# Matmuls of one array form put side by side, and the last weights and half of the output taken by column halves, in a kernel of windowed attention and soft experts

## The chip, the cores and the metric

The kernel runs on one core of one Trainium2 chip. A core has a matrix engine (TensorE, PE in the profile; its weight loads are the row PEld), a vector engine (VectorE, DVE), a scalar engine (ScalarE, ACT), a general engine (GpSimd, POOL) and SyncE (SP). Each works through its own list of instructions in order and waits on semaphores of the others. Matrix results go to PSUM, 8 banks of 512 float32 columns on 128 partitions; everything else lies in SBUF. Sixteen DMA engines move data between HBM and SBUF; loads are issued by GpSimd here (they turn float32 into float16 on the way), stores by SyncE. The metric is the device time of one execution in microseconds, the median of several runs.

## What is computed

Causal attention in a window of 64 keys (8 batches, 8 heads, 576 positions, 64 columns a head), and then a soft mixture of 8 experts with 4 slots each over the 4,608 rows of 512 that the attention gives. Cut to what matters:

```python
scores = scale * np.matmul(q, k.transpose(0, 1, 3, 2))
rel = pos[:, None] - pos[None, :]
scores = np.where((rel >= 0) & (rel < 64), scores, -1000000000.0)
attn = softmax(scores, axis=-1)
x = np.matmul(attn, v)                      # rows: 8 * 576, columns: 8 heads * 64
logits = x @ phi                            # [4608, 32]
d = softmax(logits, axis=0)                 # over all rows
slot_input = (d.T @ x).reshape(8, 4, 512)
for e in range(8):
    slot_out[e] = np.maximum(slot_input[e] @ w1[e], 0.0) @ w2[e]
c = softmax(logits, axis=1)
out = c @ slot_out.reshape(32, 512)
```

The inputs are float32: q, k and v 9.4 MB each, w1 and w2 16.8 MB each, and the output 9.4 MB.

## The kernel before, in words

The order of every engine is the order in which the program is written (`manual_schedule`), so what the code says first is done first on its engine.

**Attention.** The work is cut into 32 pairs of heads, p = 0 to 31, four pairs a batch. A loop over n = -1 to 30 ("slots", L515 to L585) works on several pairs at once, each in a different stage: the transposes of q of pair n and of k of pair n + 1 (`st_transpose`, L280), the row maxima of pair n - 1 (`st_max`, `st_max8`, L303 to L319), scores and exponentials of pair n - 2 (`st_scores`, L328 and L330; `st_score`, L335; `st_exp8`), products with v of pair n - 3 (`st_av`, L352) with their division (`st_norm`), transposes of the result of pair n - 4 (`fr_transpose`, L376). At the slot's end `st_shift` (L322) turns the maxima of pair n - 1, with 9 columns of m as its weights, and VectorE copies the rows into rt. ScalarE copies the turned k and q out of PSUM (L287, L292). Once a batch come the logits (`fr_logits`, L390), the running softmax over rows (`fr_max`, `fr_exp`, `fr_stat`), the slot sums (`fr_dispatch`, `fr_slots`, `fr_acc`) and the softmax over slots (`cb_max`, `cb_sub`, `cb_exp`, `cb_sum`, `cb_mul`, `cb_turn`), of which `cb_sub` and `cb_mul` run on GpSimd.

**Forms on TensorE.** A product with 128 weight columns uses the whole array. Products with 64 weight columns (the transposes of q and k, `st_av`) use half of its columns, those with 32 (logits, slots, experts) a quarter; the 9 columns of `st_shift` take a quarter too. The profile writes the form as rows*columns, such as 128*64.

**Loads.** All come from GpSimd, in one order (`loads`, L497): k, q and v in groups of two pairs (288 KB as float16), and the weights of experts 0 to 6, first matrices w1 (i = 0 to 6) and then second matrices w2 (i = 7 to 13), 1 MB each, by the table WSLOTS at L491: 12 of them in the loop, at n = 8i/3. v is copied once more by GpSimd, shifted by 64 rows (`shift_v`, L159 and L161), as soon as it has landed. Expert 7 has no place of its own: its first matrix is loaded in four quarters into buffers of q (`load_last1`, w1h), its second in four quarters into buffers of k (`load_last2`, w2h), each quarter two blocks of rows with all 512 columns.

**The tail** (from L618). After the loop the last pairs are finished. GpSimd there executes, in this order: the last w1h, `shift_v(15)`, the weights 12 and 13, four w2h, and `make_ss4` (L601), which writes a constant matrix ss4. `spread(b)` (L607) multiplies ss4 with the softmax over slots of batch b; `spread(0)`, in the middle of the tail, is followed on ScalarE by its copy and then by `fr_exp` of the last batch. Then come the last slot sums, and `first(g, f2)` (L741) multiplies the slot inputs by w1 of four experts at a time, `turn_hidden` turns the result, and `second(g, fcs)` (L763) multiplies it by w2, experts 0 to 3 (g = 0), then 4 to 7 (g = 1), into one PSUM bank `op`.

**The output.** ScalarE copies `op` to SBUF (osb, L806). Then, for each k of four quarters of the rows (two batches each), 9 products of 128 rows with 512 columns (L820) are copied out of PSUM by ScalarE and VectorE in turn (L821) and stored by SyncE (L823), three at a time, the first three singly. A partition's 9 rows lie one behind another in HBM.

Of the kernel before, what the change touches and what calls it, by code (L numbers as in the profile page):

```python
# [18 lines left out]
def kernel(  # L19
# [114 lines left out]
    def load_last2():  # L134
        i = len(w2_t[last])
        c = pin.tile([128, 2, D], FP16, name="w2h", tag="ks")
        nc.gpsimd.dma_start(out=c, in_=w2_dram(last)[:, i // 4, i % 4:i % 4 + 2, :])
        w2_t[last].extend(c[:, j, :] for j in range(2))
# [43 lines left out]
    NK, NQ = 3, 3  # L182
# [26 lines left out]

    make_rt(rts[0])  # L210
    zero_q(1)
    wm = const.tile([128, 5, 128], FP16, name="wm")
# [16 lines left out]
    phi_f = const.tile([128, NKK, NSLOT], FP32, name="phi_f")  # L229
# [41 lines left out]
    mts, xbs, pts, xts = {}, {}, {}, {}  # L271
# [14 lines left out]
    def st_copy_k(p):  # L286
        nc.scalar.activation(kTs[p % NK][:, 64:64 + S], turned(a_kh), AF.Copy, scale=QKS)  # L287
# [12 lines left out]
    def st_max(p):  # L300
        m = pw.tile([128, 10], FP16, name="m", tag="m")
# [6 lines left out]
        nc.vector.reduce_max(m[:, 0:8].rearrange("p (l c) -> p l c", l=2),  # L308
                             a_m[:, :, :].rearrange("p l (c x) -> p l c x", x=128), axis=AXX)
        mts[p] = m  # L310
# [7 lines left out]
    def st_max8_read(p, m8=m8):  # L318
        nc.vector.reduce_max(mts[p][:, 8:9], m8, axis=AXX)  # L319

    def st_shift(p, t_=a_v[64:64 + NB, 1, 384:512]):
        nc.tensor.matmul(t_, mts.pop(p)[:, 0:NB], ident_h[:, :], start=True, stop=True, skip_group_check=True)  # L322
        nc.vector.tensor_copy(out=rts[p % NR][64:64 + NB, :], in_=t_)  # L323
# [8 lines left out]
    def st_score(p):  # L332
        pt = pw.tile([128, NB, 128], FP16, name="pt", tag="pt")
        st_scores(p, range(8), lambda i: a_s[:, i // 4, 128 * (i % 4):128 * (i % 4) + 128])
        nc.scalar.activation(pt[:, 0:8, :].rearrange("p i x -> p (i x)"), a_s[:, :, :], AF.Exp, scale=XS)  # L335
        pts[p] = pt

    s8 = a_k[:, 288:416]

    def st_exp8(p):  # L340
        nc.scalar.activation(pts[p][:, 8, :], s8, AF.Exp, scale=XS)
# [62 lines left out]
    def fr_turn(b):  # L404
        pool = pw if b < B - 1 else pmo
        lgT = pool.tile([128, 6, 32], FP32, name="lgT", tag="lgT")
        nc.vector.transpose(lgT[:, :, :].rearrange("p i s -> p (i s)"), lgq[b][:, :])
        lgs[b] = lgT
# [15 lines left out]

    def cb_max(b):
# [10 lines left out]
    def cb_exp(b):  # L436
        pool = pw if b < B - 1 else pmo
        ec = pool.tile([128, 6, 32], FP32, name="ec", tag="lgec")
# [10 lines left out]
    def cb_mul(b, eng):  # L449
        ec, rs = cbs[b]  # L450
        pool = pw if b < B - 1 else pmo
        cc = pool.tile([128, 6, 32], FP16, name="cc", tag="cc")
# [35 lines left out]
    WSLOTS = {8 * i // 3: i for i in range(12)}  # L488
# [26 lines left out]
    for n in range(-1, NP - 1):  # L515
# [4 lines left out]
        if of(n, 17) is not None:  # L520
            cb_mul(of(n, 17), nc.gpsimd)

        if live(n - 1):
            st_max(n - 1)
            st_max8(n - 1)
        if live(n - 3):
# [3 lines left out]

        if live(n):
            st_transpose(n, "qs", a_qh)
            st_copy_q(n)
        if n == 0:
            masks_by_key()

        if sb is not None:
            fr_dispatch(sb)
            fr_dispatch_copy(sb)
        if live(n - 3):  # L540
            st_norm(n - 3)
        if sb is not None:
            fr_stat(sb)
        if eb is not None:
            fr_max(eb)

        if live(n - 2):
            st_score(n - 2)
        if live(n - 2):
            st_scores(n - 2, (8,), lambda i: s8)  # L550

        if sb is not None:
            fr_acc(sb, fr_slots(sb))
# [6 lines left out]

        if lb is not None:
            fr_logits(lb)
        if live(n - 4):
            fr_transpose(n - 4)
        if lb is not None:
            fr_logits_copy(lb)
        if live(n - 4):
            fr_transpose_copy(n - 4)
        if eb is not None:
            fr_exp(eb)  # L570
        if of(n, 15) is not None:
            cb_exp(of(n, 15))

# [52 lines left out]
    for i in range(12, 2 * NRES):  # L626
        load_w(i)
    for i in range(4):
        load_last2()
# [6 lines left out]
    st_shift(p - 1, a_k[64:64 + NB, 128:256])  # L636
# [6 lines left out]
    st_score(p - 1)  # L643
    st_max8(p, m8k)
# [4 lines left out]
    st_shift(p, a_m[64:64 + NB, 1, 384:512])  # L649
# [6 lines left out]
    st_score(p)  # L656
    st_scores(p, (8,), lambda i: s8)
# [68 lines left out]
    psr = ctx.enter_context(tc.tile_pool(name="psr", bufs=1, space=bass.MemoryType.PSUM))  # L726
    pex = ExitStack()
    psh = pex.enter_context(tc.tile_pool(name="psh", bufs=5, space=bass.MemoryType.PSUM))
    pso = pex.enter_context(tc.tile_pool(name="pso", bufs=1, space=bass.MemoryType.PSUM))
# [6 lines left out]
    op = pso.tile([128, D], FP32, name="op")  # L736
# [26 lines left out]
    def second(g, fcs):  # L763
        for fc in fcs:
            for j in range(4):
                nc.tensor.matmul(op[32 * j:32 * j + 32, :], hT[g][:, fc, 32 * j:32 * j + 32],
                                 w2_t[4 * g + j][fc], start=(g == 0 and fc == 0),
# [19 lines left out]
    second(0, range(4))  # L787
# [6 lines left out]
    second(0, range(4, 8))  # L794
# [5 lines left out]
    second(1, range(8))  # L800
# [5 lines left out]
    act(out=osb, in_=op[:, :])  # L806
    pex.close()
    obs = [w1_t[e, 0][:, 0:3, :].rearrange("p c f -> p (c f)").bitcast(FP32).rearrange("p (c d) -> p c d", d=D)
           for e in range(NRES)]
    pst = ctx.enter_context(tc.tile_pool(name="pst", bufs=2, space=bass.MemoryType.PSUM))  # L810
# [43 lines left out]
```

## Time and profile before

| what | value |
| --- | --- |
| runs | 195.84, 197.09, 197.68 us; median 197.09 |
| profiled execution | 196.56 us, its span 194.5 us, mean granted clock 0.962 |
| PE busy | 165.9 us, 85% of the span |
| ACT, DVE, POOL busy | 141.7, 137.0, 101.6 us |
| DMA | 40.87 MB as written, mean 210 GB/s; HBM read 61.93 MB, written 9.44 MB |
| chain that ended last | DMA 48%, POOL 13%, issue 10%, PE 9%, DVE 7%, ACT 5% |
| load of one weight (1,024 KB) | 16.0 us from issue to landing, median |
| k, q, v group (288 KB) | 10.7, 14.6, 12.8 us |
| last w2h issued, landed | 146.82, 164.31 us |
| first store issued | 166.65 us |

All times inside an execution count from the start of its span. The row DMA of the page's slices is the mean busy share of the sixteen engines; GB/s counts what is written, so a load of float32 that arrives as float16 counts half of what is read. The chain is followed back from the last instruction, each step to what released it. "Issue to landing" of a load includes the time in which it lies in the queue behind earlier ones. In a timeline a line is one group of instructions, with start, duration, engine, source line, operation, out<-in and shapes; a bracket tells how long the engine stood idle before it, and what ended that.

### The profile page before, as it was taken

The page shows a single profiled execution, that of the slowest core. Times are in us where ns is not written, and L with a number is a line of the kernel's source. Part 1 is how long each engine was busy: PE and PEld are TensorE (multiplying, and loading weights), DVE is VectorE, ACT ScalarE, POOL GpSimd, SP SyncE. Part 2 cuts the span into 40 slices and gives each one's busy share as a digit, 9 for nine tenths or more (in the row PEclk, how much of TensorE's full clock was granted, in tenths as well). Part 3 has the DMA queues.
Part 4 walks back from the last instruction along what each step waited for, and adds up shares of the span by engine and source line. Part 5 has one row for each costly group of instructions (what it writes and reads, how often), then busy time and mean ns, then how long its engine had stood idle before and what let it go on. Part 6 is the DMA issues. An engine that isn't in the chain of part 4 may idle for free.

```text
span 194.5 us, 6770 instructions
## 1 busy us (share of the span) xinstructions
PE 165.9 (85%) x2925; PEld 119.0 (61%) x2925; DVE 137.0 (70%) x325; ACT 141.7 (73%) x256; POOL 101.6 (52%) x131
## 2 busy tenths in 40 slices
PE   5599999979999999999999999999999898666100
PEld 1367878767777687777777777777785454232000
DVE  6676676857767877878887897878687756687400
ACT  4558878869788978979897987889878445556100
POOL 7959908289473736986456598547294133000000
PEclk9979999999999999999999999999999999999855
DMA  5999999999999999999999999999999993499993
GB/s 66 161 175 185 226 180 220 177 194 210 183 223 178 222 179 196 208 184 219 183 211 187 190 209 187 211 192 203 201 206 212 212 207 63 162 385 413 411 421 153
DMA packets 56573, 40.87 MB, mean 210 GB/s; under 512 B 38752, under 2 KB 51040, under 8 KB 55648
## 3 DMA queue, kind: packets, MB, share of 16 engines
q0 software_dynamic: 54000, 30.94, 113.3%
q1 hardware_dynamic: 2544, 9.50, 12.2%
q8 instruction: 23, 0.38, 0.7%
q14 instruction: 6, 0.05, 0.1%
HBM read 61.93 MB, written 9.44 MB: 367 GB/s over the span
## 4 chain that ended last, share of the span: by engine, by line
DMA 48%; POOL 13%; issue 10%; PE 9%; DVE 7%; ACT 5%; POOLq 0%; DVEq 0%; ACTq 0%
DMA v<-in_v_dram 31%; DMA w2h<-in_moe_w_dram 9%; DMA w<-in_moe_w_dram 6%; DVE w L821 5%; POOL v L161 3%; PE cp L820 3%; DMA qs<-in_q_dram 3%; POOL v L152 3%; POOL v L159 2%; POOL ks L79 2%; ACT qb L292 2%; PE a_m L306 1%; POOL qs L79 1%; PE a_m L303 1%; DVE m L308 1%
## 5 line engine op out<-in xcount | busy, mean ns | idle before, releaser
L292 ACT ACTIVATE qb<-a_q 64x576 f16<-64x576 f16 x64 | 41.3, 645 | 18.6 <-PE a_q L280 18.2
L308 DVE TENSOR_REDUCE m<-a_m 128x8 f16<-128x1024 f32 x32 | 39.2, 1224 | 12.6 <-PE a_m L306 12.1
L159 POOL COPY v<-v 64x1152 f16<-64x1152 f16 x16 | 18.3, 1141 | 42.9 <-DMA v<-in_v_dram 42.6
L335 ACT ACTIVATE pt<-a_s 128x1024 f16<-128x1024 f32 x32 | 32.8, 1024 | 1.1
L362 DVE TENSOR_TENSOR x_b<-a_v,rc 128x640 f16<-128x640 f32 x31 | 25.6, 824 | 1.1
L306 PEld LDWEIGHTS <-qb 128*128 128x128 f16 x256 | 17.2, 99 | 8.3 <-ACT qb L292 1.0
L287 ACT ACTIVATE kT<-a_k 128x576 f16<-128x576 f16 x32 | 20.9, 654 | 0.8 <-PE a_k L280 0.8
L380 ACT COPY xt<-a_q 128x576 f16<-128x576 f16 x31 | 20.4, 657 | 0.2 <-PE a_q L376 0.2
L306 PE MATMUL a_m<-kT,qb 128*128 128x128 f16 x256 | 19.9, 221 | 0.1
L152 POOL DMA_DIRECT2D v<-in_v_dram x16 | 19.9, 1241 | 0.0
L328 PE MATMUL a_s<-rt,lh 128*128 128x128 f16 x256 | 19.8, 220 | 0.0
L303 PE MATMUL a_m<-wm,ident_h 128*128 128x512 f16 x64 | 19.8, 391 | 0.0
L330 PE MATMUL a_s<-qb,kT 128*128 128x128 f16 x256 | 19.5, 219 | 0.0
L330 PEld LDWEIGHTS <-kT 128*128 128x128 f16 x288 | 18.8, 98 | 0.0
L328 PEld LDWEIGHTS <-lh 128*128 128x128 f16 x288 | 17.6, 98 | 1.7
L161 POOL COPY v<-v 64x1088 f16<-64x1088 f16 (+1 forms) x16 | 17.9, 1119 | 0.8
L323 DVE CAST rt<-a_v 9x128 f16<-9x128 f32 x30 | 8.7, 289 | 13.5 <-PE a_v L322 13.3
L280 PE MATMUL a_q<-ident_h,qs 96*64 96x96 f16 x384 | 14.8, 209 | 3.8 <-DMA qs<-in_q_dram 1.9
L352 PE MATMUL a_v<-v,pt 128*64 128x65 f16 x558 | 15.7, 197 | 1.4 <-POOL v L161 1.2
L280 PEld LDWEIGHTS <-qs 96*64 96x64 f16 x384 | 12.7, 111 | 5.7 <-issue 3.4
L352 PEld LDWEIGHTS <-pt 128*64 128x64 f16 x576 | 12.7, 110 | 4.6 <-issue 1.2
L280 PE MATMUL a_k<-ident_h,ks 96*64 96x96 f16 x384 | 14.8, 214 | 0.3 <-DMA ks<-in_k_dram 0.3
(162 smaller groups left out, 309.9 us busy)
## 6 DMA issues: line engine op xcount, KB each, us to landing
w<-in_moe_w_dram POOLq DMA_DIRECT2D x14, 1024.0 KB, 16.0
out_dram<-w SPq DMA_DIRECT2D x11, 768.0 KB, 8.1
qs<-in_q_dram POOLq DMA_DIRECT2D x16, 288.0 KB, 14.6
v<-in_v_dram POOLq DMA_DIRECT2D x16, 288.0 KB, 12.8
ks<-in_k_dram POOLq DMA_DIRECT2D x15, 288.0 KB, 10.7
w1h<-in_moe_w_dram POOLq DMA_DIRECT2D x4, 256.0 KB, 13.0
w2h<-in_moe_w_dram POOLq DMA_DIRECT2D x4, 256.0 KB, 17.3
out_dram<-w SPq DMA_DIRECT2D x3, 256.0 KB, 2.3
```

The costliest lines, as they stand in the source:

```text
L152: nc.gpsimd.dma_start(out=v1s[b % 2][:, c, 0:Dh], in_=v[b].rearrange("h s d -> (h s) d").rearrange("(c p) d -> p c d", p=128)[:, c, :])
L159: nc.gpsimd.tensor_copy(out=v2[64:128, c0:c1, 0:Dh], in_=v1[0:64, c0:c1, 0:Dh])
L161: nc.gpsimd.tensor_copy(out=v2[0:64, c0:c1, 0:Dh], in_=v1[64:128, c0 - 1:c1 - 1, 0:Dh])
L280: nc.tensor.transpose(tq[64 * hf:64 * hf + 64, RP * r:RP * r + RP], src[0:RP, h + hf, Dh * r:Dh * r + Dh], ident_h[0:RP, 0:RP])
L292: nc.scalar.activation(qbs[p % NQ][h, :, hf, :], turned(a_qh)[h], AF.Copy, scale=QKS)
L306: nc.tensor.matmul(a_m[:, i // 4, 128 * (i % 4):128 * (i % 4) + 128], qblock(p, i), kwindow(p, i), start=False, stop=True, skip_group_chec ...
L308: nc.vector.reduce_max(m[:, 0:8].rearrange("p (l c) -> p l c", l=2), a_m[:, :, :].rearrange("p l (c x) -> p l c x", x=128), axis=AXX)
L328: nc.tensor.matmul(at(i), lh[:, i, :], rt[:, :], start=(i % 4 == 0), stop=False, skip_group_check=True)
L330: nc.tensor.matmul(at(i), kwindow(p, i), qblock(p, i), start=False, stop=True, skip_group_check=True)
L335: nc.scalar.activation(pt[:, 0:8, :].rearrange("p i x -> p (i x)"), a_s[:, :, :], AF.Exp, scale=XS)
L352: nc.tensor.matmul(a_v[r0:r0 + 64, hf, 65 * (i // 2):65 * (i // 2) + 65], pt[:, i, 64 * hf:64 * hf + 64], rhs, start=True, stop=True, skip ...
L362: nc.vector.tensor_tensor(out=xbs[b][:, :, 128 * hp:128 * hp + 128].rearrange("p c (l d) -> p l c d", l=2), in0=avv[:, :, :, 0:64], in1=rc ...
```

## The change

In the loop the order of a slot's products is new. First come `fr_max`, `st_max` and `st_max8`, the score of the ninth block (now `st_score8`) and `fr_dispatch`; then the half-column products, `st_av`, the transposes of k and those of q; then (once a batch) the logits; and then whole ones, `st_score`, `fr_transpose` and `st_shift`, with `fr_slots` between them once a batch. `st_shift` takes all 128 columns of a wider m, whose other columns are zeros, so that it too uses the whole array. There are four buffers of kT instead of three, and every fourth k copy (p = 5, 9, ... 29) goes from ScalarE to VectorE. phi is first loaded into the place of w1 of expert 6, and some small tiles of the last batch lie in the place of lh.

The loop loads 10 weights, at n = 10i/3; the weights 10 to 12 come in the tail. The second matrix of expert 6 and that of expert 7 are loaded by column halves, in two pieces a half each: both experts' left halves, then both right halves. `second` works on one column half d at a time, in one PSUM bank each, first the experts 0 to 3 of both halves, then 4 and 5 of both, then 6 and 7. After 6 and 7 of the left half, the left half of the output of the first two quarters of the rows is computed and stored, then the right half in the same way; the other two quarters follow with whole rows.

```diff
-    def load_last2():
-        i = len(w2_t[last])
-        c = pin.tile([128, 2, D], FP16, name="w2h", tag="ks")
-        nc.gpsimd.dma_start(out=c, in_=w2_dram(last)[:, i // 4, i % 4:i % 4 + 2, :])
-        w2_t[last].extend(c[:, j, :] for j in range(2))
+    DH = D // 2
+    def load_half(d):
+        for h in range(2):
+            nc.gpsimd.dma_start(out=w2_t[last - 1, 0][:, 4 * h:4 * h + 4, DH * d:DH * d + DH],
+                                in_=w2_dram(last - 1)[:, h, :, DH * d:DH * d + DH])
+        w2_t[last].append([])
+        for h in range(2):
+            c = pin.tile([128, 4, DH], FP16, name="w2h", tag="ks")
+            nc.gpsimd.dma_start(out=c, in_=w2_dram(last)[:, h, :, DH * d:DH * d + DH])
+            w2_t[last][d].extend(c[:, j, :] for j in range(4))
...
-    NK, NQ = 3, 3
+    NK, NQ = 4, 3
...
-    phi_f = const.tile([128, NKK, NSLOT], FP32, name="phi_f")
+    phi_f = w1_t[NRES - 1, 0][:, 0, 0:2 * NKK * NSLOT].bitcast(FP32).rearrange("p (c s) -> p c s", s=NSLOT)
...
-        nc.scalar.activation(kTs[p % NK][:, 64:64 + S], turned(a_kh), AF.Copy, scale=QKS)
+        if p % 4 == 1 and p > 1:
+            nc.vector.tensor_scalar(out=kTs[p % NK][:, 64:64 + S], in0=turned(a_kh), scalar1=QKS, scalar2=None,
+                                    op0=ALU.mult)
+        else:
+            nc.scalar.activation(kTs[p % NK][:, 64:64 + S], turned(a_kh), AF.Copy, scale=QKS)
...
-    def st_shift(p, t_=a_v[64:64 + NB, 1, 384:512]):
-        nc.tensor.matmul(t_, mts.pop(p)[:, 0:NB], ident_h[:, :], start=True, stop=True, skip_group_check=True)
-        nc.vector.tensor_copy(out=rts[p % NR][64:64 + NB, :], in_=t_)
+    def st_shift(p, t_=a_v[:, 1, 384:512]):
+        nc.tensor.matmul(t_, ms[p % 2][:, :], ident_h[:, :], start=True, stop=True, skip_group_check=True)
+        nc.vector.tensor_copy(out=rts[p % NR][64:64 + NB, :], in_=t_[64:64 + NB, :])
...
-    WSLOTS = {8 * i // 3: i for i in range(12)}
+    WSLOTS = {10 * i // 3: i for i in range(10)}
...
-    for i in range(12, 2 * NRES):
+    for i in range(10, 2 * NRES - 1):
         load_w(i)
-    for i in range(4):
-        load_last2()
+    for d in range(2):
+        load_half(d)
     make_ss4()
...
-    psh = pex.enter_context(tc.tile_pool(name="psh", bufs=5, space=bass.MemoryType.PSUM))
+    psh = pex.enter_context(tc.tile_pool(name="psh", bufs=4, space=bass.MemoryType.PSUM))
...
-    def second(g, fcs):
-        for fc in fcs:
-            for j in range(4):
-                nc.tensor.matmul(op[32 * j:32 * j + 32, :], hT[g][:, fc, 32 * j:32 * j + 32],
-                                 w2_t[4 * g + j][fc], start=(g == 0 and fc == 0),
+    def second(d, g, js=range(4)):
+        for fc in range(NFC):
+            for j in js:
+                nc.tensor.matmul(ops[d][32 * j:32 * j + 32, 0:DH], hT[g][:, fc, 32 * j:32 * j + 32],
+                                 w2_at(4 * g + j, d, fc), start=(g == 0 and fc == 0),
...
+    def give(k, e0, ne, c0, nc_):
+        nonlocal turn, piece
         ov = out[2 * S * k:2 * S * k + 2 * S, :].rearrange("(p e) d -> p e d", e=NE)
...
+        for i0 in range(0, ne, n1):
+            n_ = min(n1, ne - i0)
+            cp = pst.tile([128, n1, nc_], FP32, name="cp", tag="cp")
...
+            (act, dve)[turn % 2](out=ob[:, i0:i0 + n_, :], in_=cp[:, 0:n_, :])
             turn += 1
...
+        nc.sync.dma_start(out=ov[:, e0:e0 + ne, c0:c0 + nc_], in_=ob)
+    second(0, 1, (2, 3))
+    act(out=osb[:, 0:DH], in_=ops[0][:, 0:DH])
+    for k, e0, ne in ((0, 0, 2), (0, 2, 2), (0, 4, 5), (1, 0, 4), (1, 4, 5)):
+        give(k, e0, ne, 0, DH)
+    second(1, 1, (2, 3))
+    act(out=osb[:, DH:D], in_=ops[1][:, 0:DH])
+    for k, e0, ne in ((0, 0, 4), (0, 4, 5), (1, 0, 4), (1, 4, 5)):
+        give(k, e0, ne, DH, DH)
+        spread(4 + 2 * k + e0 // 4, (act, dve)[turn % 2])
+    for k in range(2, B // 2):
+        for e0 in range(0, NE, 3):
+            give(k, e0, 3, 0, D)
```

## The prediction

> **What bounds the kernel now.** I read the page's slices first.
>
> ```profile
> PE   5599999979999999999999999999999898666100
> DMA  5999999999999999999999999999999993499993
> GB/s 66 161 175 185 226 180 220 177 194 210 183 223 178 222 179 196 208 184 219 183 211 187 190 209 187 211 192 203 201 206 212 212 207 63 162 385 413 411 421 153
> ```
>
> Each digit is 4.86 us. TensorE and the DMA engines are both full from about 5 to 160 us: the loads are a full pipe beside a full TensorE. Only near 160 to 170 us does the pipe run empty, before the output drains at about 410 GB/s. The chain of waits, from the last loads on:
>
> ```profile
> 134.53 12.01 DMA w<-in_moe_w_dram
> 146.53 0.28 issue
> 146.82 17.50 DMA w2h<-in_moe_w_dram
> 164.31 0.04 issue
> 164.36 0.61 PE op L766 x5
> 164.96 0.02 issue
> 164.99 0.59 ACT qb L806
> ```
>
> The end is set by the last load (164.31), but hardly: TensorE waited only 0.25 us for it. The first two lines matter more: a load issued at 134.53 lands at 146.53, and only then is the last w2h issued. The timeline of GpSimd (start, duration, what) shows the same:
>
> ```profile
> 142.84 1.41 POOL L122 DMA_DIRECT2D w<-in_moe_w_dram  x2
> 144.25 1.63 POOL L137 DMA_DIRECT2D w2h<-in_moe_w_dram  x3
> 146.82 0.54 POOL L137 DMA_DIRECT2D w2h<-in_moe_w_dram  x1 [0.94 <-DMA w<-in_moe_w_dram]
> 147.34 0.55 POOL L602 MEMSET v<- 128x512 f16 x1
> 147.95 1.33 POOL L605 COPY v<-ss 32x128 f16<-32x128 f16 x4
> ```
>
> GpSimd stood still for 0.94 us before its fourth w2h. The load that released it is the eighth before it in GpSimd's own order (w, w1h, w1h, w, w, three w2h). At 51.75 us a w load waits 0.47 us in the same way, for a q load eight before it. So at most eight of GpSimd's loads are under way; the ninth waits until the first has landed, and all of GpSimd waits with it. Behind these issues stand L602 and L605, make_ss4, ended at 149.28. The timeline of TensorE then has
>
> ```profile
> 148.97 0.42 PE L390 MATMUL a_s<-xt,phi_sb 128*32 128x128 f16 x8
> 149.31 0.43 PE L612 MATMUL a_v<-ct_all,v 128*128 128x128 f16 x5
> ```
>
> L612 is spread(0), which reads ss4: it starts 0.03 us after ss4 is complete. Whatever delays ss4 now delays TensorE, and all of the tail is behind it.
>
> **The change, part by part.** *Sorted products.* Same-form 128x128 matmuls start 56 ns apart; the start after a change of form comes 138 to 154 ns later, as in
>
> ```profile
> 88.26 0.45 PE L376 MATMUL a_q<-ident_h,x_b 128*128 128x128 f16 x5
> 88.64 0.22 PE L322 MATMUL a_v<-ident_h,m 128*9 128x128 f16 x1
> 88.80 0.61 PE L303 MATMUL a_m<-wm,ident_h 128*128 128x512 f16 x2
> ```
>
> (five starts at 56 ns would let L322 begin at 88.54; it begins at 88.64). A slot has six such changes (before and after L322; max to attention-value; transposes to score; score to k transposes; those to L376) and will have two. Four times about 95 ns is 0.38 us a slot of 4.37 us (the mean between the starts of L303), some 11 us over 30 slots. ScalarE gives up 7 k copies (0.65 us each), VectorE takes them. The loop then ends near 138 us instead of 149. This gain ends at spread(0), and what is late next there is ss4.
>
> *Weights in the loop: 10 instead of 12, five loads' worth behind it instead of three.* The same bytes cross the same full pipe; q, k and v only come earlier by two weights. Landings of a 1 MB weight are 4.9 us apart (154.4, then 159.3). Take w_5, the second matrix of expert 5. Ahead of it stand, before and after, the same loads: all of q, k, v, seven first matrices, w_0 to w_4 of the second, four w1h. In a full queue it lands when it landed before. It is the load issued at 142.84:
>
> ```profile
> DMA to landing us min/median/max: 11.6/11.6/11.6
> ```
>
> that is at 154.4. Take 154.4, with ends of 153.4 and 155.9 (uneven landings of the last loads).
>
> *Eight quarter loads instead of four.* After w_5, GpSimd issues w6a, w6a, w7a, w7a, w6b, w6b, w7b, w7b (experts 6 and 7, a and b the column halves). The eighth of them is the ninth load counted from w_5, and in the compiled order of the changed kernel it does wait on the semaphore that w_5 updates (the seventh on that of w_4). make_ss4 stays behind it. So GpSimd resumes at 154.4 + 0.29 (146.53 to 146.82), issues for 0.52, and make_ss4 takes 1.94 (147.34 to 149.28): ss4 is complete at 157.15 instead of 149.28. **spread(0) is 7.9 us later.** TensorE, done with attention at about 138, stands idle until then; ScalarE is queued behind spread(0)'s copy, with fr_exp of the last batch after it; GpSimd's cb_sub and cb_mul follow too.
>
> *Clock.* The granted clock was 0.50 at 10 to 12 us, after TensorE had been busy 0.48 of 2 us at 6 to 8, and L303's pair took 1.01 us there against 0.60. After some 18 us of idling spread(0) will meet that clock. The stretch from spread(0) to the first expert (149.31 to 155.18) holds about 3.7 us of matmuls that the path waits for. At half clock they cost up to 3.7 more; none if the clock returns at once. I take 2.5, as the slow stretch at the start lasted 3.4 us. The Trainium skill, "TensorE: Matmul & The Clock Gate", Part 1, says that an idle window of about 3.4 us halves the clock and a busy one restores it; by that rule alone 3.4 to 6.8 us would be slow and the term 2 to 3.7 us. The start of this trace agrees.
>
> *Second matrices by halves.* second(0) has the same columns. second(1) becomes three runs of about 0.9 us before half 0 is complete (pairs of experts, 16 matmuls of 256 columns), against two runs of 0.86: half 0 ends at 162.42 + 2.6 + 0.2 of latency = 165.2 on the old axis, against 164.97. **+0.2.** Its halves cover themselves: pieces of 768-byte runs (q, k) land 1.5 us apart for 288 KB, those of 128-byte runs (v) 2.0, so a 256 KB piece in 512-byte runs takes 1.33 to 1.8; half 0 is in by 159.7 to 161.6, half 1 by 168.8 at most, and they are wanted after 174.
>
> *First output.* 256 columns are copied from PSUM instead of 512, then one bank: about 1.35 us instead of 1.66 (164.99 to 166.65). **-0.3.**
>
> *Output.* Half of it now leaves in 1 KB runs. In the DMA records of the trace an output packet of 2,048 bytes takes 87 ns, one of 6,144 takes 240. By size alone 1 KB would be 43, no loss; by the ratio of the loads' 768- and 2,048-byte packets (80 and 173 ns) 50. At 48 ns, 4,608 packets on 16 engines are 13.8 us, against 11.7 for the same rows now: **+2.0** (0 to 2.6). By the Trainium skill, "DMA: Bandwidth & Descriptors", Specifications, 512 bytes are enough for line rate; by it this term would be 0 and the sum 2 us less. The trace's 87 ns against a third of 240 speaks for some loss already at 2 KB. Against this, the rows for 169 to 171 us show 217 and 227 GB/s instead of 410 (0.9 us lost to late copies); with four banks in turn **-0.8**.
>
> *No cost:* phi's place in w_6 (read at slot 5, loaded over at slot 20), the wider m and the fourth kT (the loop would have to lose 18 us to reach the path).
>
> Sum against the profiled run (span 194.5 us, 196.56 with what lies around it; the median of the three is 0.5 higher): 7.9 + 2.5 + 0.2 - 0.3 + 2.0 - 0.8 = 11.5, so **208.0 us**. With the ends: 196.56 + (6.9 + 0 + 0.2 - 0.3 + 0 - 1.0) = 202.4 and 196.56 + (9.4 + 4 + 0.2 - 0.3 + 2.6 + 0) = 212.5.
>
> **Rivals.** *1. The output starts under the last loads, and it is faster.* If ss4 were ready early, half 0 would be bound by its weights (159.7); first issue 161.6, first bytes 162.3, then 2.7 us left of the second halves, 24.9 of output (167.4 to 191.2 today, less 0.9, plus 2.0) and 3.3 to the end of the span: 193.2, or 195.3 us; if loads hide wholly under writes, 192.6. For it: the empty 164 to 167 us. Against it: the wait on w_5. It decides if the held issue waits for something that lands by about 146 us, w_3 rather than w_5.
>
> *2. The queue runs dry as well.* If the slots stay at 4.37 us (a latency or VectorE's k copies undo the gain), the last w1h still waits for TensorE until 139.1, while the queue, two weights shorter, empties at about 137.6 (the last v lands at 140.4 - 9.8; a w1h, a weight and a w1h follow, 1.2 + 4.9 + 1.2). Then shift_v (2.3), an issue, its way (1.7) and three weights: w_5 lands at 139.7 + 4.0 + 14.7 = 158.4, and all is some 4 us later: 212 us. Against it: the cost of a change of form is measured, and 0.1 us a slot brings that w1h to 136.
>
> *3. Sorting buys nothing on TensorE:* the same as rival 2 in time.
>
> **How the numbers follow.** Forecast 0.76, rivals 2 and 3 0.12, rival 1 0.09, 0.03 unplaced. Point 208, the forecast's. The range 202.4 to 212.5 is the forecast's own with both ends, and holds most of rival 2; rival 1 and the tails are left out, under 2 in 10. About 1% is what a measurement of this kernel can tell from no change (its runs span 195.84 to 197.68). Rival 1 divides into 0.05 faster and 0.04 same; of the unplaced, 0.01 each: faster 0.06, same 0.05, slower 0.89.
>
> **What would show it.** In the timeline of GpSimd a wait of some 10 us or more on a w load before the last w2h, ended at 154 to 155; make_ss4 after it; TensorE idle before spread(0) with Pool as releaser, and a granted clock of 0.5 there; the loads ended long before the first output. Starts of L303's successor near 4.0 us apart would show the sorting. I am wrong if the last w2h is issued before 148 us, or if writes and w2h loads overlap.

## The result, and the profile after

| | before | after |
| --- | --- | --- |
| median | 196.81 us (195.84 to 197.68, 4 runs) | 223.53 us (223.1 to 224.0, 4 runs) |
| ratio, 95% interval | | 1.136 (1.130 to 1.142) |
| span of the profiled execution | 194.5 us | 221.3 us |
| mean start to start of a slot, slots 4 to 28 | 4.37 us | 4.67 us |
| last w1h issued | 139.10 us | 149.59 us |
| w_5 (second matrix of expert 5) landed | 154.4 us | 171.29 us |
| ss4 complete | 149.28 us | 174.23 us |
| first store issued | 166.65 us | 193.35 us |
| first store to the end of the span | 27.85 us | 27.95 us |

The change is slower, as forecast, but by 26.7 us where 11.5 were forecast; the time lies 11 us above the upper end of the range. The page's slices of the kernel after (each digit 5.53 us) show the place:

```profile
PE   6599887889878788977988888899800599988300
PEclk9999999999999999999999999999955569999855
DMA  5999999999999999999999994396999990099996
GB/s 81 158 174 207 196 184 211 186 218 184 202 193 182 212 187 213 181 191 203 147 174 159 153 172 65 53 170 84 198 215 203 196 123 3 3 299 338 376 415 280
```

Two things are new beside the hole that was forecast (PE 00 near 160 to 171 us, the clock at half there and behind it, then a DMA hole while the experts run). TensorE stands mostly at 7 and 8 through the loop where it stood at 9. And the loads run dry before the loop is over: 65 and 53 GB/s from 133 to 144 us. The timeline of GpSimd (start, duration, engine, line, operation; in the bracket the idle time before it, and what ended that):

```profile
140.72 0.60 POOL L131 DMA_DIRECT2D w1h<-in_moe_w_dram  x1 [0.75 <-PE a_q L294]
141.31 0.72 POOL L122 DMA_DIRECT2D w<-in_moe_w_dram  x1
149.59 0.55 POOL L131 DMA_DIRECT2D w1h<-in_moe_w_dram  x1 [7.57 <-PE a_q L294]
150.19 1.14 POOL L169 COPY v<-v 64x1152 f16<-64x1152 f16 x1
151.38 1.14 POOL L171 COPY v<-v 64x1152 f16<-64x1152 f16 x1
152.47 2.13 POOL L122 DMA_DIRECT2D w<-in_moe_w_dram  x3
154.58 1.50 POOL L139 DMA_DIRECT2D w<-in_moe_w_dram  x2
156.07 1.48 POOL L144 DMA_DIRECT2D w2h<-in_moe_w_dram  x2
157.54 0.74 POOL L139 DMA_DIRECT2D w<-in_moe_w_dram  x1
161.52 0.74 POOL L139 DMA_DIRECT2D w<-in_moe_w_dram  x1 [3.24 <-DMA w<-in_moe_w_dram]
166.74 0.74 POOL L144 DMA_DIRECT2D w2h<-in_moe_w_dram  x1 [4.48 <-DMA w<-in_moe_w_dram]
171.58 0.74 POOL L144 DMA_DIRECT2D w2h<-in_moe_w_dram  x1 [4.10 <-DMA w<-in_moe_w_dram]
172.31 0.54 POOL L628 MEMSET v<- 128x512 f16 x1
172.91 1.32 POOL L631 COPY v<-ss 32x128 f16<-32x128 f16 x4
```

A w1h is a quarter of the first matrix of expert 7, a w a whole weight (L122) or a piece of half of expert 6's second matrix (L139), a w2h such a piece of expert 7's (L144). The lower half is the forecast stall: three of the eight pieces each wait for the load eight before them. These are w_3, w_4 and w_5, which landed at 160.74, 166.44 and 171.29, about 0.3 to 0.8 us before each issue; and make_ss4 stands behind them. The upper half is what was not forecast. The last w1h needs a buffer that the q transposes (L294) release, and they come so late that GpSimd waits 7.57 us for them, with three whole weights behind it in its list and only one weight left in the queue (issued at 141.31, landed at 152.26). The view of waits (who <- whom: us in total, times, longest) shows both ends of it:

```profile
PE a_q L401 <- ACT qb L310: 13.8, 21, 0.9
PE a_v L638 <- POOL v L631: 13.3, 1, 13.3
POOL w1h L131 <- PE a_q L294: 13.2, 4, 7.6
```

The second row is spread(0) waiting for ss4. The first is the loss in the loop: 21 times the transposes of the attention result wait for the copies of q. A slot's middle in the timeline of TensorE, and ScalarE at the same time:

```profile
84.07 0.61 PE L347 MATMUL a_s<-qb,kT 128*128 128x128 f16 x8
85.52 0.44 PE L401 MATMUL a_q<-ident_h,x_b 128*128 128x128 f16 x5 [0.84 <-ACT qb L310]
```

```profile
83.65 0.64 ACT L305 ACTIVATE kT<-a_k 128x576 f16<-128x576 f16 x1
84.18 1.29 ACT L310 ACTIVATE qb<-a_q 64x576 f16<-64x576 f16 x2
```

The q transposes fill bank a_q, and the result's transposes overwrite it. Before, the score, the ninth block and the k transposes stood between the two writes in TensorE's list, and ScalarE copied q first and k behind the score. Now only the score lies between, 16 starts at 56 ns or 0.90 us, and ScalarE copies k before the two halves of q. The copies end at 85.47, L401 starts at 85.52.

What the sorting did to TensorE itself is read from the busy times of the stretch 60 to 130 us, before and then after (the last row of the view by windows, four windows together):

```profile
sum 70.00, PE 68.97 PEld 53.29 DVE 57.01 ACT 61.40 POOL 44.67; mean PE 17.24 PEld 13.32 DVE 14.25 ACT 15.35 POOL 11.17
```

```profile
sum 70.00, PE 58.68 PEld 47.27 DVE 54.27 ACT 56.09 POOL 42.83; mean PE 14.67 PEld 11.82 DVE 13.57 ACT 14.02 POOL 10.71
```

Four slots take 17.43 us before and 18.86 on average after (18.7 or 19.0), so the 70 us hold 16.06 and 14.85 slots. TensorE works 4.29 us a slot before and 3.95 after: 0.34 of the 0.38 that the forecast priced is there. But it stands idle for 0.06 us a slot before and for 0.76 after, so that a slot grows by 0.36. Of the 11.3 us of idle in this stretch the view of waits names 6.8 as waits of L401 for the q copies (11 times), 2.9 as waits of L401 for the copy of the logits, which lies in the same bank (4 times), and 1.2 as waits of L321 for fr_acc on VectorE (4 times).

### The profile page after: what moved, and what is told of

It is laid out like the page before. It is cut to its first block, busy times and chain, and to the rows that moved or that the text cites. A ratio compares the mean times of both kernels' runs of the same rounds, so it can differ in the third digit from the quotient of the medians.

```text
span 221.3 us, 6986 instructions
## 1 busy us (share of the span) xinstructions
PE 163.9 (74%) x3007; PEld 123.3 (56%) x3007; DVE 142.0 (64%) x346; ACT 140.7 (64%) x263; POOL 105.0 (47%) x134
## 4 chain that ended last, share of the span: by engine, by line
PE 35%; ACT 19%; DMA 14%; DVE 12%; issue 10%; POOL 4%; DVEq 0%; ACTq 0%; POOLq 0%
ACT qb L310 11%; DMA w<-in_moe_w_dram 8%; PE a_m L321 5%; PE a_m L324 5%; PE a_v L377 4%; ACT kT L305 3%; DMA out_dram<-w 3%; PE a_k L294 3%; PE a_q L401 3%; DVE x_b L387 3%; DMA ks<-in_k_dram 2%; PE op L796 2%; ACT pt L366 2%; DVE m L326 2%; PE a_k L616 2%
## 5 line engine op out<-in xcount | busy, mean ns | idle before, releaser
L310 ACT ACTIVATE qb<-a_q 64x576 f16<-64x576 f16 x64 | 41.1, 642 | 5.7 <-PE a_q L294 3.2
L401 PE MATMUL a_q<-ident_h,x_b 128*128 128x128 f16 x155 | 13.7, 218 | 18.2 <-ACT qb L310 13.8
L366 ACT ACTIVATE pt<-a_k 128x128 f16<-128x128 f32 x32 | 8.9, 277 | 26.3 <-PE a_k L294 19.4
L401 PEld LDWEIGHTS <-x_b 128*128 128x128 f16 x160 | 11.2, 96 | 22.5 <-issue 22.0
L321 PE MATMUL a_m<-wm,ident_h 128*128 128x512 f16 x64 | 19.9, 394 | 1.7 <-DVE acc L512 1.5
L324 PE MATMUL a_m<-kT,qb 128*128 128x128 f16 x256 | 20.4, 225 | 0.1
L345 PE MATMUL a_s<-rt,lh 128*128 128x128 f16 x256 | 20.3, 223 | 0.0
L405 ACT COPY xt<-a_q 128x576 f16<-128x576 f16 x31 | 19.7, 635 | 0.2 <-PE a_q L401 0.2
L347 PE MATMUL a_s<-qb,kT 128*128 128x128 f16 x256 | 19.6, 220 | 0.0
L347 PEld LDWEIGHTS <-kT 128*128 128x128 f16 x288 | 19.0, 99 | 0.0
L294 PE MATMUL a_q<-ident_h,qs 96*64 96x96 f16 x384 | 15.9, 213 | 2.6 <-DMA qs<-in_q_dram 2.6
L305 ACT ACTIVATE kT<-a_k 128x576 f16<-128x576 f16 x25 | 16.1, 645 | 2.2 <-PE a_k L294 2.2
L294 PE MATMUL a_k<-ident_h,ks 96*64 96x96 f16 x384 | 16.2, 215 | 0.1
```

Source lines behind the costliest of these rows:

```text
L294: nc.tensor.transpose(tq[64 * hf:64 * hf + 64, RP * r:RP * r + RP], src[0:RP, h + hf, Dh * r:Dh * r + Dh], ident_h[0:RP, 0:RP])
L310: nc.scalar.activation(qbs[p % NQ][h, :, hf, :], turned(a_qh)[h], AF.Copy, scale=QKS)
L321: nc.tensor.matmul(a_m[:, j, :], ident_h[:, :], wm[:, j:j + 4, :].rearrange("p c x -> p (c x)"), start=True, stop=False, skip_group_check= ...
L324: nc.tensor.matmul(a_m[:, i // 4, 128 * (i % 4):128 * (i % 4) + 128], qblock(p, i), kwindow(p, i), start=False, stop=True, skip_group_chec ...
L345: nc.tensor.matmul(at(i), lh[:, i, :], rt[:, :], start=(i % 4 == 0), stop=False, skip_group_check=True)
L347: nc.tensor.matmul(at(i), kwindow(p, i), qblock(p, i), start=False, stop=True, skip_group_check=True)
```

## The experiments

The theory from the traces (T1): the new order of a slot makes TensorE wait for ScalarE, so the loop is slower. With two weights fewer in the loop the queue runs empty, the last w1h is issued late, and w_5 with it. ss4 then waits for w_5 (eight loads under way). The rivals: VectorE's share of the k copies slows the slots; the pipe is full and the table does not matter; the halves and 1 KB stores cost the time. Unless a run below says otherwise, its edit is to the changed kernel. Each is one execution with a profile, but for e10 and e11, and each is compared with a run of the kernel before on the same chip (196.55 to 197.27).

**e1: make_ss4 ahead of the loads.**

```diff
     st_transpose(p, "qs", a_qh)
+    make_ss4()
     load_last1()
...
         load_half(d)
-    make_ss4()
```

> The changed kernel with make_ss4 put ahead of the tail's last loads, nothing else. If the eight-loads limit holds ss4 and ss4 holds TensorE: the 13.3 us wait before spread(0) is gone, and with it the half clock; TensorE reaches spread(0) near 160 us, half 0 is then bound by its weights, which land at 176.6 as in the changed kernel (the loads do not move), first store near 179 instead of 193.4, and the rest (28 us from the first store to the end, plus the 3 us of right halves still to be loaded) gives a span of 207 to 211, a time of 209 to 213 us. If something else holds the tail, the time stays at 223.

Measured: 206.87 us, span 205.1, 2 us below what was expected. The loop is as slow as it was (4.67), w_5 lands at 169.28; GpSimd's three waits on weights are all still there, but nothing that TensorE waits for stands behind them, and the granted clock stays full until 195.1 us. The first store is issued at 176.80. So the place of make_ss4 behind the loads is worth 16.7 us of the 26.7, and 10 us have another cause.

**e2: slots in the order of before.** The loop body is that of the kernel before, every k copy on ScalarE; the table of 10, the halves, the wide m of `st_shift` and the late ss4 stay.

```diff
         if live(n - 3):
             st_av(n - 3)
         if live(n - 1):
             st_max8_read(n - 1)
-        if n == 0:
+        if live(n):
             st_transpose(n, "qs", a_qh)
             st_copy_q(n)
...
-        if live(n) and n > 0:
-            st_transpose(n, "qs", a_qh)
```

> The changed kernel with the loop's order of the kernel before, and all k copies on ScalarE; the tail, the load table, the halves and the wide m stay. If the new order in the slot is what slows the loop: slots back at 4.37 us (or a little less, as the wide m saves two changes of form, 0.2 us), the last w1h waits until about 139 (or 133), w_5 lands at 155 to 159 instead of 171.3, and the time is 207 to 212 us. If the loop is slowed by the load table or by the tail: slots stay near 4.67 and the time near 223.

Measured: 213.91 us, span 212.1, w_5 at 160.61, first store at 184.11. The slots are back at 17.41 us for four; the shift in whole-array form, alone, gains 0.02 in four slots. Yet this shift takes two of the four changes of form out and leaves the order as it was. TensorE's busy time in 60 to 130 us does fall, from 68.97 to 66.82 us or by 0.14 us a slot (two changes were priced at 0.19), but TensorE then waits, where the kernel before showed no wait:

```profile
PE a_q L294 <- ACT xt L405: 2.7, 8, 0.3
```

So in the old order, too, TensorE's work alone did not set the length of a slot. Bank a_q holds the transposes of the result, ScalarE's copy of them (xt) has to end before the q transposes may overwrite them, and ScalarE copies q after that. The kernel before already has it, in three of four slots, though its view of waits is empty:

```profile
89.82 0.66 ACT L380 COPY xt<-a_q 128x576 f16<-128x576 f16 x1
89.89 0.50 PE L352 MATMUL a_v<-v,pt 128*64 128x65 f16 x18
90.53 0.45 PE L280 MATMUL a_q<-ident_h,qs 96*64 96x96 f16 x12
```

The copy ends at 90.48, the q transposes start 0.05 us later. Of the time since the products with v, 0.50 us count as busy, so only 0.14 us of idling are left to see.

The new order of the slots costs 9.6 us in this setting. The time lies 2 us above what was expected, since even at the old pace the queue runs dry, as GpSimd's timeline shows:

```profile
138.79 0.55 POOL L131 DMA_DIRECT2D w1h<-in_moe_w_dram  x1 [7.30 <-PE a_q L294]
139.39 1.14 POOL L169 COPY v<-v 64x1152 f16<-64x1152 f16 x1
140.58 1.14 POOL L171 COPY v<-v 64x1152 f16<-64x1152 f16 x1
141.67 2.13 POOL L122 DMA_DIRECT2D w<-in_moe_w_dram  x3
```

The last w1h goes out when it did before the change (139.10), but up to w_5 three weights are behind it instead of one, and by then the one load ahead of it is about to land.

**e3: the result's transposes ahead of the attention-value products.**

```diff
+        if live(n - 4):
+            fr_transpose(n - 4)
+            fr_transpose_copy(n - 4)
         if live(n - 3):
             st_av(n - 3)
...
             fr_stat(sb)
-        if live(n - 4):
-            fr_transpose(n - 4)
-            fr_transpose_copy(n - 4)
```

The logits move up with them, ahead of the transposes.

> The changed kernel with the transposes of the attention result (and the logits before them) moved to the front of the slot, ahead of the products with v; the number of changes of form stays as in the changed kernel, or one more in the slot with logits. If TensorE waits because these transposes share PSUM bank a_q with those of q, whose two copies of 1.2 us come just before them in the changed order: the wait of 0.84 us a slot for qb goes, slots fall to 3.9 to 4.2 us, w_5 lands at 154 to 157 and the time is 205 to 209 us, with the wait on ss4 still there. If ScalarE or VectorE is simply full: slots stay above 4.5 and the time at 218 to 224.

Measured: 224.61 us, w_5 at 172.15, slots 4.73 on average: missed by 16 us. L401's wait for the q copies is gone, and slots without batch work fall to 3.6 to 4.1, but the slots with it grow to 5.7 to 5.8. New waits stand there: `st_max` for fr_acc, `st_shift` for the division on VectorE, the maxima for the q copies of the same slot. Time and slots are those given for a full ScalarE or VectorE, but neither works all the time: 56.0 and 54.2 us of the 70 from 60 to 130 us. Taking one wait out of the order puts another in.

**e4: all k copies on ScalarE.**

```diff
-        if p % 4 == 1 and p > 1:
+        if False:
             nc.vector.tensor_scalar(out=kTs[p % NK][:, 64:64 + S], in0=turned(a_kh), scalar1=QKS, scalar2=None,
```

> The changed kernel with all k copies on ScalarE again. If the bank a_q and the q copies set the pace: a copy of k of 0.54 us stands before the q copies in one slot more of four, so that slots grow by up to 0.13 us on average and the time is the same or up to 5 us more (223 to 228). If VectorE, with its seven k copies, sets the pace: slots fall to 4.3 or 4.4 us and the time to 210 to 214.

Measured: 223.89 us, slots 4.67, L401's wait 14.3 us (13.8). VectorE's k copies are not the cause.

**e5: q turned and copied before k.** In the sorted slot the logits and the q transposes come first, then exp8 and the q copies, then the k transposes, the dispatch copy and the k copy.

```diff
-        if live(n + 1):
-            st_transpose(n + 1, "ks", a_kh)
+        if lb is not None:
+            fr_logits(lb)
+        if live(n) and n > 0:
+            st_transpose(n, "qs", a_qh)
         if live(n - 2):
             st_exp8(n - 2)
-        if live(n + 1):
-            st_copy_k(n + 1)
...
         if live(n) and n > 0:
             st_copy_q(n)
         if lb is not None:
             fr_logits_copy(lb)
+        if live(n + 1):
+            st_transpose(n + 1, "ks", a_kh)
+        if sb is not None:
+            fr_dispatch_copy(sb)
+        if live(n + 1):
+            st_copy_k(n + 1)
```

> The changed kernel with another order inside the half-column part of a slot: logits, q transposes and their copies first, then k transposes and the k copy; the dispatch copy ahead of the k copy. The transposes of the attention result stay behind the scores, on bank a_q. If their wait for the q copies (0.84 us a slot) slows the loop: the q copies now run beside k transposes and scores (1.4 us), the wait falls under 0.2 us, slots fall from 4.67 to 3.8 to 4.1 us, the queue stays full, w_5 lands at 154 to 157, and the time is what was forecast for the changed kernel, 204 to 210 us, with ss4 still held until w_5 has landed. If the loop is slowed by something else in the new order: slots above 4.4, time 216 to 224.

Measured: 217.78 us, w_5 at 165.24, first store at 188.00. One slot in its timeline of TensorE:

```profile
63.00 0.61 PE L347 MATMUL a_s<-qb,kT 128*128 128x128 f16 x8
63.75 0.44 PE L401 MATMUL a_q<-ident_h,x_b 128*128 128x128 f16 x5
```

The end of L347 to L401 shrinks from 0.84 to 0.14 us, and a slot without batch work from about 4.4 to 3.7. That is the wait of T1, most of it taken out: ScalarE's q copies now end at 63.70, and from the last start of L347 to L401 there are still 0.36 us where products of one form follow each other at 0.056. The batch slots stay long (5.02 and 5.15), since they wait for other things: 0.47 us for the logits' copy, 0.40 for fr_acc. Four slots take 17.97 us, still more than the 17.43 of the order before. Of the 13 to 19 us expected, 5.7 came, and the time lies where it was put for a loop slowed by something else as well.

**e6 and e7: e5 and e2, each with make_ss4 ahead of the loads** (the edit of e1).

> The same, with make_ss4 ahead of the tail's last loads. If both causes are what I take them for, they add: TensorE passes spread(0) before 145 us; GpSimd is still held by the last two loads until w_5 has landed (155), ScalarE waits there for cb_sub of batch 5, then some 7 us to half 0; first store near 163, time 193 to 197 us. If the stall on ss4 was hiding another one as long: 203 us or more.

> The changed kernel with the slot order of the kernel before (as in the second experiment: 213.9 us, w_5 at 160.6, left halves in at 166) and make_ss4 first. If ss4 is the tail's only hold: half 0 is bound by its weights at 166 and TensorE's own chain at 165 to 167, first store at 168 to 169, time 197 to 200 us. If the lane wait also costs through cb_sub and cb_mul: up to 204.

Measured: e6 202.52 us (w_5 164.83, last piece of half 0 at 170.19, first store 172.36), e7 198.65 us (160.85, 166.22, 168.39). e7 is as expected; e6 is 5.5 us above, because the loop of e5 is too slow for it (w_5 was expected at 155). In both, the first store follows the last piece of half 0 by 2.17 us, and in e1 too (174.63, 176.80): with ss4 out of the way the loads set the end, and they follow the pace of the loop.

**e8: the kernel before, with make_ss4 ahead of its loads** (the same edit).

> The kernel before with make_ss4 ahead of its tail's loads. In its profile ss4 was complete 0.03 us before TensorE used it, and its wait on the eighth load back was 0.94 us. If ss4 was just in time there: no gain, 196 to 197 us. If it already held TensorE: up to 1 us faster.

Measured: 197.11 us, beside it 197.27. In the kernel before, ss4 was just in time.

**e9: the load table of before.**

```diff
-    WSLOTS = {10 * i // 3: i for i in range(10)}
+    WSLOTS = {8 * i // 3: i for i in range(12)}
...
-    for i in range(10, 2 * NRES - 1):
+    for i in range(12, 2 * NRES - 1):
```

> The changed kernel with 12 weights in the loop again (n = 8i/3) instead of 10; slots, halves and make_ss4 behind the loads as changed. Theory (the slots set when the last w1h is issued, and the queue is empty by then): slots stay at 4.67, the last w1h is issued near 149 as before, but one weight instead of three stands between it and the quarters, so w_5 lands where w_3 landed, at 161 to 163 instead of 171.3; the span is w_5 + 50 to 51.5, the time 213 to 216. Rival (the pipe is full, the same bytes take the same time wherever the table puts them, and something else held w_5): w_5 stays at 170 to 172, 222 to 225 us.

Measured: 211.58 us, span 209.8, slots 4.67, last w1h issued at 148.07, w_5 at 158.98. The theory holds in kind; w_5 lands 2 us earlier than it said, and the time is 1.4 us below its range. The rival of the full pipe falls: the table alone is worth 12.0 us. With e2 and the two kernels this fills a table of when w_5 landed:

| | 12 weights in the loop | 10 weights in the loop |
| --- | --- | --- |
| slots of before, 17.4 us for four | 154.4 | 160.61 (e2) |
| slots of the change, 18.7 to 19.0 us for four | 158.98 (e9) | 171.29 |

The pace alone makes it 4.6 us later, the table alone 6.2, both 16.9: 6.1 more than the sum (4.1 by e1, where w_5 landed at 169.28 with the slots and the table of the change). The bytes ahead of w_5 are about the same in all four; from 100 us to its landing the engines moved them at 201 GB/s before, at 177 in e2 and in e9, and at 153 after the change. My reading is that a full queue absorbs a part of either delay, and that little is left to absorb the second one once the first has emptied it.

**e10: the halves alone.** The slots of e2 and the table of e9, with make_ss4 first: the change without its new slots and table.

> The kernel before with the halves of the change, the wide shift matrix, and make_ss4 ahead of the tail's loads: slot order and load table of before. It is what the change would be without the sorted slots and the new table. Theory: w_5 lands at 154 to 156 as before, w7a by 160 to 161.5, half 0 is then bound by TensorE, not by loads; first store 166 to 166.7, 28.5 to the end: span 194.5 to 195.2, time 196 to 197.5, no change to be measured. Rival (my rival 1: the halves let the output start under the last loads and bring 1 to 3 us): 193.5 to 195.5. Rival (the halves cost by their 1 KB packets and small loads): 198 to 200.

Measured in 10 runs: 196.4 us, ratio to the kernel before 0.999 (0.994 to 1.003): no change. Its slices of DMA (each 4.86 us):

```profile
DMA  5999999999999999999999999999999996599997
GB/s 72 169 184 192 215 185 215 180 200 203 188 217 184 215 181 199 202 189 216 185 212 183 185 206 189 209 191 204 202 199 208 193 189 95 171 336 341 397 414 288
```

The pipe is full to the end of the loads and the hole is short. Half 0 is in at 160.38, yet the first store goes out at 166.86, as before: the chain through TensorE sets it, whose second matrices for half 0 end at 165.36. So the halves neither cost nor bring anything here; 27.64 us from the first store to the end stand against 27.85.

**e11: e10 with a sorted slot again**, in the order of e5, and what e5's batch slots waited for moved away (the diff is against e5's slot).

```diff
-        if sb is not None:
-            fr_dispatch_copy(sb)
...
+            fr_acc(sb, fr_slots(sb))
+            fr_stat(sb)
         if live(n - 2):
             st_score(n - 2)
             st_exp(n - 2)
+        if eb is not None:
+            fr_exp(eb)
...
-        nc.scalar.copy(out=lg, in_=lgps[b == B - 1])
+        (nc.vector.tensor_copy if b < B - 2 else nc.scalar.copy)(out=lg, in_=lgps[b == B - 1])
```

The dispatch copy comes right after `st_max8_read`, and `fr_max` after the division.

> e10 with a sorted slot again, in the order of e5 (q transposes ahead of k) and with the three waits left in e5 taken out: the logits' copy on VectorE instead of ScalarE, the slot sums (fr_slots, fr_acc) ahead of the scores instead of behind them, fr_max and fr_exp behind the division. If the waits on the other engines are all that kept the sorted order from its 0.4 us a slot, TensorE's steady slots fall to 4.1 to 4.3 (16.4 to 17.2 us per batch, 17.4 before), spread(0) and the first store come 2 to 6 us earlier where the loads allow it (w7a by 160 gives a first store by 162.5), 192 to 195.5 us. If ScalarE or VectorE then sets the pace anyway, slots stay at 4.35 to 4.5 and the time is 196 to 199.

Measured in 4 runs: 207.02 us, ratio 1.055 (1.051 to 1.060): both expectations missed. Its view of waits of TensorE, for 60 to 130 us:

```profile
PE a_v L339 <- DVE x_b L387: 4.8, 4, 1.2
PE a_k L294 <- ACT pt L366: 2.5, 4, 0.6
PE a_q L401 <- DVE lg L420: 2.1, 4, 0.5
PE a_k L489 <- ACT d L440: 1.7, 4, 0.4
```

Each repair made a wait of its own, once a batch: with the logits' copy and a k copy both on VectorE its division is 1.2 us late for `st_shift`; fr_exp, moved back, is late for the dispatch. The slots with batch work are 6.2 and 5.7 us long, the others 3.68 as in e5.

Step by step, in this order, the 26.7 us are: 223.5 after, 206.9 with ss4 first (e1: 16.7), 198.65 with the slots of before as well (e7: 8.2), 196.4 with the table of before as well (e10: 2.2, no more than single runs of one kernel differ here), and 196.6 the kernel before in the same comparison. No version here beats the kernel before by more than its runs differ.

## Why the prediction was right on the stall and wrong on the loop

**What held.** *The quarter loads and ss4.* From w_5's landing to ss4 the forecast had 0.29 + 0.52 + 1.94 = 2.75 us; it was 2.94 (an issue takes 0.74, not 0.52). TensorE idle with Pool as releaser and the half clock stand in the trace as described; the stall is three waits on w_3, w_4 and w_5 of 11.8 us in all, where I looked for one of some 10, and it ends at 171.6 instead of 154 to 155. e1 shows that make_ss4 behind it costs the 16.7 us.

*The tail.* From ss4 to the first store 17.37 us before and 19.12 after: +1.75, where clock, second matrices and first output were priced at 2.5 + 0.2 - 0.3 = 2.4. From the first store to the end +0.1 where 2.0 - 0.8 = 1.2 was priced. Its one part that can be read alone, the 1 KB packets, was about right: 48 ns each in the median of the DMA records and 49.8 on average, priced 48. The half of the output that they carry took 14.2 us (194.26 to 208.48), priced 13.8; so the rest, the smoother start above all, gave about 2.4 by difference instead of 0.8. The page named for it, the Trainium skill, "DMA: Bandwidth & Descriptors", Specifications, which has line rate from 512 bytes on, did not hold in these runs: the slices show 338 GB/s for the 1 KB runs and 415 for whole rows.

**What failed: the step "Sorted products", and with it "Weights in the loop".** The forecast took 0.38 us of TensorE's work off a slot and let the slot shrink by as much, so that the loop ends near 138 us and the queue stays full. The work did shrink, by 0.34. But the step took a TensorE that is busy for 98% of the time for the engine that sets the slot, and e2 shows that it was not: 0.14 us less work a slot in the old order made the slot no shorter, since TensorE waits there for ScalarE's copies out of bank a_q. And in the new order the slot grew by 0.36 (a quarter of 18.86 - 17.43), because the same edit moved the transposes of the result up to the copies of q, which share a PSUM bank: TensorE went from 0.06 us of idle a slot to 0.76. I had listed each form change and had not asked, for each product that moved, what now stands between its bank's last reader and itself (L401 against L310, `st_max` against `fr_acc`). The first maxima behind the loop start at 147.76 instead of 137.26, and the last w1h follows by as much.

The second half, "the same bytes cross the same full pipe", was never put to the test at the pace that it assumed, since no run reached it; it had no margin. At the old pace (e2) the queue ran dry and w_5 landed at 160.6. That is rival 2, whose 158.4 and 212 us came close to e2's 160.61 and 213.9 (its 137.6 for the empty queue adds up to 137.9 from its own terms); I gave it 0.12 because I held the 0.38 for safe. At the pace that came, it was 171.29, 16.9 us after the 154.4 of the forecast. All that follows w_5 took 50.0 us to the end of the span, where the forecast had 51.5: 16.9 - 1.5 = 15.4, the distance between 208.0 and 223.5.

**Rival 1** (the output starts under the last loads) needed an early ss4. With it and the old loop and table (e10) the time is that of before; the 195.3 that it promised lies just below e10's interval (0.994 times 196.6 is 195.5). Half 0 is in 6.5 us before the first store there, so the loads are not what the output waits for. **Rival 3** (sorting buys nothing on TensorE) falls as it was put: sorting takes 0.34 us a slot off TensorE's work. In time that bought nothing in any run here, as rival 3 had it.

What stays open: whether any order of sorted slots beats 17.4 us for four. Three were tried (the change, e3, e5) and a repair of the last (e11); the slots without batch work reach 3.6 to 3.7 us (in e3 and e5 every second one), the others always lost more.

## What to carry to other kernels

An engine that counts as busy for 98% of the time need not be the one that sets the pace: look at whether its instructions start right behind another engine's end, as the q transposes did here. A saving on it is a saving in time only if the order it needs leaves every other wait covered: for each instruction that moves, look for the last reader of the buffer or bank that it writes, and subtract the engine's work that now lies between the two. A queue that a loop keeps full hides a slower loop or a later load, but not both; where the loads behind a loop are issued by an engine that waits for the loop's buffers, price the case in which the queue is empty there. And a small instruction that something needs (make_ss4 here) does not belong behind loads on an in-order engine: moving it ahead cost nothing in the kernel before (e8) and was worth 16.7 us in the one after (e1).

## What the runs showed of the hardware

The granted clock fell sooner and came back later than the forecast had it. These are stretches of 1 us of the kernel after (start:end, length, busy time of PE, PEld, DVE, ACT and POOL, then the clock, the DMA share and GB/s):

```profile
159.00:160.00 1.00, 0.91 (x13) 0.30 (x9) 0.06 (x1) 0.59 (x1) 0.00 (x0) 1.00 1.00 201
160.00:161.00 1.00, 0.00 (x0) 0.00 (x0) 0.93 (x4) 0.00 (x0) 0.00 (x0) 0.93 1.04 209
161.00:162.00 1.00, 0.00 (x0) 0.00 (x0) 0.20 (x1) 0.00 (x0) 0.48 (x1) 0.50 1.12 229
...
173.00:174.00 1.00, 0.64 (x3) 0.27 (x3) 0.00 (x0) 0.00 (x0) 0.83 (x4) 0.50 1.45 196
...
180.00:181.00 1.00, 1.00 (x3) 0.30 (x2) 0.96 (x5) 0.51 (x1) 0.00 (x0) 0.50 0.70 99
181.00:182.00 1.00, 1.00 (x8) 0.37 (x6) 0.68 (x3) 0.27 (x1) 0.64 (x2) 0.83 0.07 9
```

TensorE's last matmul ended at 159.9, the clock was at half 1 us later, and it stayed there for 8 us after work began again at 173.25, though TensorE counts as busy for most of them. In e9, 2.56 us without work (158.4 to 160.9) were enough, and the half clock lasted from 161.4 to 171.6. The Trainium skill, "TensorE: Matmul & The Clock Gate", Part 1, gives about 3.4 us of idleness for the fall and about 3.4 us of sustained work for the return; counted from the last and the first matmul, neither fits these two traces, where the fall came after 1.0 and 3.0 us (in e9 with work already resumed) and the return after 8.1 and 10.7 us. What does fit is the length of the stretches of half clock ahead of the output: 3.41 us before and in e7 and e11, 10.24 in e9, 20.48 after and in e3 and e5, 23.89 in e2 and e4, all whole multiples of 3.41. The forecast's remark that the start of the trace before agrees holds for that length alone, for TensorE had been idle there for only 1.9 us (5.33 to 7.23). What the half clock cost is open: from ss4 to the first store 1.75 us were added in all, but which matmuls the path waited for was not taken apart.
